# Values right behind the scores, and a last chunk of tokens at full height, in a fused attention and mixer kernel

## The chip, the cores and the metric

The kernel runs on one core of a Trainium2 chip. The core has five engines with queues of their own: TensorE (PE, with its weight loads as PEld), VectorE (DVE), ScalarE (ACT), GpSimd (POOL) and SyncE (SP), which here only issues DMAs. Each engine works through its instructions in the order in which the program emits them; semaphores hold an instruction back until its inputs are there. The metric is the time of one execution in device microseconds, as the median over several runs.

## The reference

Attention with a threshold, then an MLP mixer. All results are float32; the four MLP weights arrive as float64, because a float32 array is multiplied with a float64 scalar.

```python
# q, k, v: (8, 8, 576, 64); tau = 0.02
scores = scale * np.matmul(q, k.transpose(0, 1, 3, 2))
thresh = np.max(scores, axis=-1, keepdims=True) - tau
scores = np.where(scores >= thresh, scores, -1000000000.0)
scores = scores - np.max(scores, axis=-1, keepdims=True)
attn = np.exp(scores)
attn = attn / (np.sum(attn, axis=-1, keepdims=True) + 1e-09)
x = np.matmul(attn, v)                     # then (B, H, S, D) -> (B, S, H*D) = (8, 576, 512)
...
h = np.maximum(x.transpose(0, 2, 1) @ w_tok1, 0.0) @ w_tok2     # 576 -> 256 -> 576 tokens
u = x + h.transpose(0, 2, 1)
out = u + np.maximum(u @ w_ch1, 0.0) @ w_ch2                    # 512 -> 1536 -> 512 channels
```

## The kernel before

The work is cut into 144 units: 8 batch rows, in each of them two groups of two head pairs, in each group 9 units (`t` 0 to 8). A unit is 128 query rows of one head pair; unit `t == 4` holds the last 64 query rows of both pairs. One loop (from line 524) goes over the units and emits, by hand and in this order, what each engine is to do; nothing is reordered afterwards.

In one turn of the loop for unit `u` stand:

- `scores(u)`: TensorE computes the scores of both heads into PSUM (`sc`, line 297, two matmuls in the two halves of the array at a time, shape 64*128); VectorE takes the row maximum (`mx`, line 302), GpSimd makes the bias (line 303). From row 1 on `sc` has one pair of buffers.
- `norm(u - 1)`: VectorE makes the reciprocal of the row sums (lines 321 and 322), GpSimd scales the exponentials (line 325).
- `turn_blocks(u - 2)` (from row 1 on) or `turn` (row 0): the weights of attention are transposed. In row 0 TensorE does it, with copies out of PSUM (line 350). From row 1 on VectorE transposes blocks of 32x32 (line 359), and when a group of one or two units is complete, SyncE issues 16 DMAs that move the blocks from `T` to `eT` (line 369). The group's call of `values` is then put on the list `due`, for two units later (one in row 0).
- `fill(share)`: takes steps of the two MLPs from the list `todo`, up to a share of a quota per unit. A step is a handful of matmuls and what follows them: `turn_x` (lines 423 and 424), `tok1` (433 and 434), `tok2` (440 and 444), `ch1` (462 and 463), `ch2` (474 to 484). MLP results go through PSUM tiles with two buffers.
- `weigh(u)`: ScalarE applies the threshold (line 312) and the exponential with the row sum (line 315).
- the calls of `values` that are due: TensorE multiplies `eT` with v (`pv`, lines 399 and 404, shape 128*64), ScalarE copies the result to `xT` (line 409). When the last call of a batch row is done, `push` puts that row's MLP steps on `todo` and sets the quota.
- loads of later q, k and v, and `prep`, which transposes q and k on VectorE (line 279).

Each float32 matmul appears in the trace as two instructions.

The float64 weights come as pairs of 32-bit words, in 31 pieces. A piece is loaded into one of `NRAW` areas of a tile that only later serves as `xT`, and converted by integer operations: two on ScalarE (lines 187 and 189), three on VectorE (lines 197, 201 and 205), one on GpSimd (line 211). Before, this runs as a pipeline in steps, three to a piece: step 3i emits GpSimd's addition for piece i - 1, the next load into the freed area, and VectorE's first operation on piece i; the two others emit one operation of ScalarE for piece i + 1 and one of VectorE for piece i. In row 0 `weight(1)` is called twice a unit; from row 1 on `weight(2)` three times: behind `norm`, ahead of `weigh`, and behind `values`. `need` emits what an MLP step is missing. 36 of the 93 steps fall in row 0.

The queue of SyncE holds, in the order emitted, the loads of pieces (line 172), in row 0 q and k (106), v (114), the block transfers (369) and the results (484). From row 1 on q and k are loaded from ScalarE's queue.

576 tokens are 4 chunks of 128 and one of 64. `tok1` contracts over tokens, so its fifth chunk uses 64 rows of the array (shape 64*128 at line 433).

Of the kernel before, what the change touches and what calls it, by code (L numbers as in the profile page):

```python
# [9 lines left out]
F32 = mybir.dt.float32  # L10
U32 = mybir.dt.uint32
I32 = mybir.dt.int32
# [5 lines left out]
P = 128  # L18
# [3 lines left out]
def kernel(  # L22
# [103 lines left out]
    wc1 = const.tile([P, NJ, NCC, P], F32, name="wc1")  # L126
    wc2 = const.tile([P, NJ, DM], F32, name="wc2")

    WMAX = 512
    scratch = work.tile([P, NP * 2 * S], U32, tag="xT", name="scratch")
    NRAW = 4
    raw_at = [scratch[:, 2 * WMAX * i : 2 * WMAX * (i + 1)] for i in range(NRAW)]

    def like(x, dst):
# [14 lines left out]
    for j in range(NJ):  # L152
        pieces.append((wc2[:, j, :], moe_w_ch2[P * j : P * j + P, :]))

    raws = {}

    def load_piece(i):
        if i >= len(pieces):
            return
# [5 lines left out]
        raw = raw_at[i % NRAW][0:rows, 0 : n * (2 if wide(i) else 1)].bitcast(src.dtype)  # L171
        nc.sync.dma_start(out=like(raw, dst), in_=src)
        if wide(i):
            words = raw.bitcast(U32).rearrange("p (n w) -> p n w", w=2)
            h2 = work.tile([P, WMAX], F32, tag="o", name=f"h2_{i}")[0:rows, 0:n]
            raws[i] = like(words[:, :, 0], dst), like(words[:, :, 1], dst), like(h2, dst)
        else:
            raws[i] = like(raw, dst)

    def wide(i):  # L180
        return i < len(pieces) and pieces[i][1].dtype == I64

    def on_scalar(i, part):
        if wide(i):
            lo, hi, h2 = raws[i]
            if part == 0:
                nc.scalar.activation(out=lo.bitcast(I32), in_=lo, func=AF.Copy, scale=2.0**-29)
            else:
                nc.scalar.activation(out=h2, in_=hi.bitcast(F32), func=AF.Square)

    def on_vector(i, part):
        if wide(i):
            dst = pieces[i][0]
            lo, hi, h2 = raws[i]
            bits = dst.bitcast(U32)
            if part == 0:
                nc.vector.tensor_scalar(
                    out=bits, in0=hi, scalar1=3, scalar2=0x3FFFFFFF, op0=ALU.logical_shift_left, op1=ALU.bitwise_and
                )
            elif part == 1:  # L200
                nc.vector.scalar_tensor_tensor(
                    out=bits, in0=hi, scalar=0xC0000000, in1=bits, op0=ALU.bitwise_and, op1=ALU.bitwise_or
                )
            else:
                nc.vector.scalar_tensor_tensor(out=dst, in0=h2, scalar=2.0**-30, in1=dst, op0=ALU.is_ge, op1=ALU.mult)

    def on_gpsimd(i):
        if i >= 0:
            dst = pieces[i][0]
            if wide(i):  # L210
                nc.gpsimd.tensor_tensor(out=dst.bitcast(I32), in0=dst.bitcast(I32), in1=raws.pop(i)[0].bitcast(I32), op=ALU.add)
            else:
                nc.gpsimd.tensor_copy(out=dst, in_=raws.pop(i))

    steps_done = 0

    def weight(n):

        nonlocal steps_done
        for k in range(steps_done, min(steps_done + n, 3 * len(pieces) + 1)):
            i, part = divmod(k, 3)
            if part == 0:
                on_gpsimd(i - 1)
                if i:
                    load_piece(i - 1 + NRAW)
            else:
                on_scalar(i + 1, part - 1)
            on_vector(i, part)  # L230
            steps_done = k + 1

    def need(i):

        weight(3 * i + 4 - steps_done)

    load_piece(0)
    load_qk(1, (nc.sync, nc.sync))
# [1 line left out]
    for i in range(1, NRAW):  # L240
        load_piece(i)
    load_v(1)
    on_scalar(0, 0)
    on_scalar(0, 1)

# [166 lines left out]
    def token_mlp(b):  # L412
        xT = xTs.pop(b)
        o = S * (b % 2)
        s = {}

        def turn_x(t):
            M = MT[t]
            if t == 0:
                s["x"] = work.tile([P, NT, DM], F32, tag="x", bufs=1, name=f"x_{b}")  # L420
            ps = ps_tr.tile([P, MAIN], F32, tag="tr", name=f"tx_{b}_{t}").rearrange("p (c x) -> p c x", c=NP)
            for p in range(NP):
                nc.tensor.transpose(out=ps[0:M, p, :], in_=xT[:, p, o + t * P : o + t * P + M], identity=ident)  # L423
            nc.scalar.copy(out=s["x"][0:M, t, :], in_=ps[0:M].rearrange("q p d -> q (p d)"))

        def tok1(m):
            need(2)
            if m == 0:
                s["a"] = work.tile([P, NTK, DM], F32, tag="a", bufs=1, name=f"a_{b}")
            ps = ps_mm.tile([P, DM], F32, tag="mm", name=f"t1_{b}_{m}")  # L430
            for t in range(NT):
                M = MT[t]
                nc.tensor.matmul(ps, lhsT=w1[0:M, t, P * m : P * m + P], rhs=s["x"][0:M, t, :], start=(t == 0), stop=(t == NT - 1))  # L433
# [74 lines left out]
    def push(b):  # L508
# [102 lines left out]
```

## Time and profile before

| what | value |
|---|---|
| time, median of 3 runs (lowest to highest) | 1412.02 us (1411.59 to 1416.25) |
| the profiled execution: its time, its span | 1412.02 us, 1410.2 us |
| mean granted clock of TensorE | 0.984 |
| PE busy, 0 to 50, 50 to 100, 100 to 150, 150 to 200 us | 32.5, 37.0, 33.5, 45.3 us |
| DVE busy in the same stretches | 30.7, 41.9, 42.2, 37.3 us |
| PE busy, 600 to 800 us | 199.9 us of 200 |
| chain that ended last, by engine | PE 81%, DVE 6%, SP queue 5%, DMA 3%, ACT 3% |
| block transfers eT<-T: issues, length of one issue (median), issue to landing | 1120, 588 ns, about 2 us |
| first max of unit 18 (row 1), 36 (row 2), 54 (row 3), 143 | 102.9, 277.3, 415.2, 1207.2 us |

Times in the profile are microseconds from the start of the span, unless marked ns. A line of a timeline gives the start, the length, the engine, the line of the kernel, the operation, what it writes and reads, and how many instructions were merged; in square brackets stands how long the engine was idle before and what ended that. SPq and ACTq are DMA issues in the queues of SyncE and ScalarE. Ends of matmuls are modelled, so distances between their starts are what can be compared. The span is a little shorter than the execution's time.

### The profile page before, as it was taken

To read this page: it belongs to the slowest core of one execution; us is meant where nothing else is said; L and a number is where in the kernel's file an instruction comes from. 1 tells how busy PE (TensorE), PEld (TensorE's weight loads), DVE (VectorE), ACT (ScalarE), POOL (GpSimd) and SP (SyncE) were. 2 spreads that over 40 slices of the span, in tenths; PEclk is the share of its full clock that TensorE was granted. 3 is DMA by queue.
4 is the path that set the end of the run, shared out by engine and by line. 5 is a ranking of instruction groups with operands and counts; after the bars stand their busy time and mean duration, and the time that the engine had idled before them with its cause. 6 is when DMAs were issued, how large, how long until landed. Compare 5 with 4: busy or idle time off the path is not lost.

```text
span 1410.2 us, 19481 instructions
## 1 busy us (share of the span) xinstructions
PE 1338.3 (95%) x6866; PEld 828.3 (59%) x6866; DVE 585.2 (41%) x1009; ACT 588.8 (42%) x1328; POOL 358.9 (25%) x681
## 2 busy tenths in 40 slices
PE   5767799979999999999999999999999999999998
PEld 3443556536665567565756566565656466566675
DVE  5788673344444443434333444434333443201000
ACT  5776554344445444353334344443334344220110
POOL 4566552222222222222122222212212222100000
PEclk8998999989999999999999999999999999999999
DMA  6444654443444434433333434342443433300000
GB/s 133 103 104 115 170 136 110 106 101 92 118 117 105 107 87 101 104 93 93 90 95 83 111 81 116 91 109 68 99 94 77 111 90 79 88 8 16 8 8 23
DMA packets 257376, 128.34 MB, mean 91 GB/s; under 512 B 208064, under 2 KB 221376, under 8 KB 257280
## 3 DMA queue, kind: packets, MB, share of 16 engines
q1 hardware_dynamic: 131632, 111.46, 30.0%
q10 hardware_dynamic: 125648, 15.64, 7.0%
q8 instruction: 55, 0.90, 0.3%
q14 instruction: 41, 0.34, 0.1%
HBM read 43.25 MB, written 9.44 MB: 37 GB/s over the span
## 4 chain that ended last, share of the span: by engine, by line
PE 81%; DVE 6%; SPq 5%; DMA 3%; ACT 3%; issue 1%; POOL 1%; DVEq 0%; ACTq 0%
PE c L478 27%; PE c L462 23%; PE sc L297 10%; PE pv L404 7%; SPq L369 4%; PE t L433 4%; PE t L440 3%; DVE mx L302 3%; PE pv L399 2%; DVE T L359 2%; PE tx L423 1%; DMA eT<-T 1%; PE c L474 1%; ACT e L312 1%; ACT e L315 1%
## 5 line engine op out<-in xcount | busy, mean ns | idle before, releaser
L302 DVE TENSOR_REDUCE mx<-sc 128x1 f32<-128x576 f32 x288 | 204.7, 751 | 495.2 <-PE sc L297 493.2
L462 PE MATMUL c<-xT,wc 128*128 128x256 f32 (+1 forms) x1920 | 405.7, 363 | 3.1 <-ACT g L463 1.8
L478 PE MATMUL c<-wc,g 128*128 128x512 f32 x864 | 389.5, 597 | 0.0
L462 PEld LDWEIGHTS c<-xT,wc 128*128 128x128 f32 x1920 | 331.1, 190 | 76.9 <-issue 29.6
L303 POOL TENSOR_SCALAR bias<-mx,toff 128x1 f32<-128x1 f32 x288 | 79.6, 276 | 833.5 <-DVE mx L302 779.0
L312 ACT ACTIVATE e<-sc,bias 128x576 f32<-128x576 f32 x288 | 199.2, 740 | 168.3 <-POOL bias L303 156.3
L478 PEld LDWEIGHTS c<-wc,g 128*128 128x128 f32 x864 | 157.6, 190 | 177.3 <-issue 175.6
L463 ACT ACTIVATE g<-c 128x256 f32<-128x256 f32 (+1 forms) x240 | 86.9, 363 | 383.5 <-PE c L462 372.4
L325 POOL TENSOR_SCALAR e<-e,rr 128x576 f32<-128x576 f32 x288 | 219.6, 775 | 16.6 <-DVE rr L322 4.4
L315 ACT ACTIVATE e<-e,ntau 128x576 f32<-128x576 f32 x288 | 220.2, 772 | 0.0
L297 PE MATMUL sc<-kT,qT 64*128 64x288 f32 (+1 forms) x1280 | 191.9, 435 | 14.7 <-DVE kT L279 8.7
L359 DVE STREAM_TRANSPOSE T<-e 128x1152 f32<-128x1152 f32 x126 | 172.5, 1369 | 15.8 <-DMA eT<-T 10.0
L297 PEld LDWEIGHTS sc<-kT,qT 64*128 64x128 f32 (+1 forms) x1280 | 104.8, 179 | 95.7 <-issue 51.1
L404 PE MATMUL pv<-eT,lv 128*64 128x256 f32 x1024 | 125.8, 389 | 0.0
L483 DVE COPY o<-c 128x512 f32<-128x512 f32 x36 | 24.6, 684 | 192.6 <-PE c L478 192.6
L404 PEld LDWEIGHTS pv<-eT,lv 128*64 128x64 f32 x1024 | 76.5, 141 | 38.3 <-issue 2.8
L440 PE MATMUL t<-w,a 128*128 128x288 f32 x256 | 78.0, 434 | 13.9 <-DVE xT L444 12.1
L433 PE MATMUL t<-x,w 128*128 128x512 f32 (+1 forms) x160 | 74.9, 606 | 0.0
L409 ACT COPY xT<-pv 128x256 f32<-128x256 f32 x64 | 23.8, 372 | 115.1 <-PE pv L404 114.9
L440 PEld LDWEIGHTS t<-w,a 128*128 128x128 f32 x256 | 46.9, 197 | 38.4 <-DVE xT L444 17.0
L444 DVE TENSOR_TENSOR xT<-xT,t 128x288 f32<-128x288 f32 x64 | 27.9, 441 | 97.5 <-PE t L440 97.4
L315 ACT ACTIVATION_READ_ACCUMULATOR e<-e,ntau 128x1 f32 x288 | 57.0, 198 | 0.0
(46 smaller groups left out, 600.9 us busy)
## 6 DMA issues: line engine op xcount, KB each, us to landing
eT<-T SPq DMA_DIRECT2D x896, 72.0 KB, 2.1
scratch<-in_moe_w_ch_dram SPq DMA_DIRECT2D x24, 512.0 KB, 3.8
lv<-in_v_dram SPq DMA_DIRECT2D x32, 288.0 KB, 3.3
out_dram<-o SPq DMA_DIRECT2D x36, 256.0 KB, 2.2
eT<-T SPq DMA_DIRECT2D x224, 36.0 KB, 1.9
lk<-in_k_dram ACTq DMA_DIRECT2D x108, 72.0 KB, 2.7
lq<-in_q_dram ACTq DMA_DIRECT2D x104, 72.0 KB, 2.1
lq<-in_q_dram SPq DMA_DIRECT2D x24, 72.0 KB, 3.3
```

What stands on the lines that cost most here:

```text
L297: nc.tensor.matmul(sc[h][rows, f, 0:HS], lhsT=qT[r, cols], rhs=kT[r, HS * f : HS * f + HS], start=True, stop=True)
L302: nc.vector.tensor_reduce(out=mx[:, c], in_=sc[h][:, :, 0:HS], axis=AX.XY, op=ALU.max)
L312: nc.scalar.activation(out=eh, in_=sc[h][:, :, 0:HS], func=AF.Prelu, bias=bias[:, h : h + 1], scale=SCALE, alpha=STEEP)
L315: nc.scalar.activation(out=eh, in_=eh, func=AF.Exp, bias=ntau, accum_out=rs[:, h : h + 1])
L325: nc.gpsimd.tensor_scalar(out=eh, in0=eh, scalar1=rr[:, h : h + 1], scalar2=1.0, op0=ALU.mult, op1=ALU.mult)
L359: nc.vector.transpose(out=T.rearrange("p (a c n x) -> p c a n x", a=4, c=NK, n=n)[:, :, :, place, :], in_=e.rearrange("p (c a x) -> p c a ...
L404: nc.tensor.matmul(to[r], lhsT=lv[:, j, :], rhs=eT[:, j], start=False, stop=(c == NI - 1), skip_group_check=True)
L433: nc.tensor.matmul(ps, lhsT=w1[0:M, t, P * m : P * m + P], rhs=s["x"][0:M, t, :], start=(t == 0), stop=(t == NT - 1))
L440: nc.tensor.matmul(ps, lhsT=s["a"][:, m, P * c : P * c + P], rhs=w2[:, m, HS * f : HS * f + HS], start=(m == 0), stop=(m == NTK - 1))
L462: nc.tensor.matmul(ps, lhsT=wc1[:, j, c, :], rhs=uT[:, c, GR * i : GR * i + n], start=(c == 0), stop=(c == NCC - 1))
L463: nc.scalar.activation(out=s["g"][:, j, 0:n], in_=ps, func=AF.Relu)
L478: nc.tensor.matmul(flat, lhsT=s["g"][:, j, P * t : P * t + P], rhs=wc2[:, j, :], start=False, stop=(j == NJ - 1), skip_group_check=True)
```

## The change

Three things change.

1. From row 1 on, the calls of `values` that are due are emitted directly behind `scores(u)`, by the new function `mix`. In row 0 they stay where they were.
2. The result of `turn_x` goes to a tile `x_sb` that lasts for the whole kernel and whose fifth chunk is zero in its lower 64 rows; `w1` gets zeros there too. `tok1` contracts all five chunks over 128 rows. Two memsets on GpSimd write these zeros at the start.
3. The conversion of weights is a generator: all operations of a piece belong to its own three steps (ScalarE's two with VectorE's first; VectorE's second; VectorE's third, GpSimd's addition and the next load). It works in two scratch areas and one for the squares, in the same tile, with three areas for raw loads in place of four. In row 0 there are still two steps a unit; from row 1 on four ahead of `weigh` and three at the end, none behind `norm`.

```diff
+    x_sb = const.tile([P, NT, DM], F32, name="x_sb")
+    nc.gpsimd.memset(x_sb[LAST:P, NI, :], 0.0)
+    nc.gpsimd.memset(w1[LAST:P, NI, :], 0.0)
...
-    NRAW = 4
+    NRAW = 3
+    a_at = [scratch[:, 2 * WMAX * NRAW + WMAX * i : 2 * WMAX * NRAW + WMAX * (i + 1)] for i in range(2)]
+    sq_at = scratch[:, 2 * WMAX * NRAW + 2 * WMAX : 2 * WMAX * NRAW + 3 * WMAX].bitcast(F32)
...
+    def f64_to_f32(dst, raw, rows, n):
+        lo, hi = raw[:, :, 0], raw[:, :, 1]
+        a = a_at[turn_of[0] % 2][0:rows, 0:n]
+        h2 = sq_at[0:rows, 0:n]
+        turn_of[0] += 1
+        af = a.bitcast(F32)
+        nc.scalar.activation(out=lo.bitcast(I32), in_=lo, func=AF.Copy, scale=2.0**-29)
+        nc.scalar.activation(out=h2, in_=hi.bitcast(F32), func=AF.Square)
+        yield nc.vector.tensor_scalar(
+            out=a, in0=hi, scalar1=3, scalar2=0x3FFFFFFF, op0=ALU.logical_shift_left, op1=ALU.bitwise_and
+        )
+        yield nc.vector.scalar_tensor_tensor(
+            out=a, in0=hi, scalar=0xC0000000, in1=a, op0=ALU.bitwise_and, op1=ALU.bitwise_or
+        )
+        nc.vector.scalar_tensor_tensor(out=af, in0=h2, scalar=2.0**-30, in1=af, op0=ALU.is_ge, op1=ALU.mult)
+        nc.gpsimd.tensor_tensor(
+            out=dst.bitcast(I32), in0=like(a.bitcast(I32), dst), in1=like(lo.bitcast(I32), dst), op=ALU.add
+        )
...
+    def weight_ops():
+        for i, (dst, src) in enumerate(pieces):
+            raw, rows, n = raws.pop(i)
+            if src.dtype == I64:
+                for _ in f64_to_f32(dst, raw.bitcast(U32).rearrange("p (n w) -> p n w", w=2), rows, n):
+                    yield
...
+            if i + NRAW < len(pieces):
+                load_piece(i + NRAW)
+            yield
...
-    on_scalar(0, 0)
-    on_scalar(0, 1)
...
-            nc.scalar.copy(out=s["x"][0:M, t, :], in_=ps[0:M].rearrange("q p d -> q (p d)"))
+            nc.scalar.copy(out=x_sb[0:M, t, :], in_=ps[0:M].rearrange("q p d -> q (p d)"))
...
-                M = MT[t]
-                nc.tensor.matmul(ps, lhsT=w1[0:M, t, P * m : P * m + P], rhs=s["x"][0:M, t, :], start=(t == 0), stop=(t == NT - 1))
+                nc.tensor.matmul(ps, lhsT=w1[:, t, P * m : P * m + P], rhs=x_sb[:, t, :], start=(t == 0), stop=(t == NT - 1))
...
+    def mix(u):
+        while due and due[0][0] <= u:
+            _, b, p, c = due.popleft()
+            values(b, p, c)
+            if p == NP - 1 and c == 1:
+                push(b)
...
         if on:
             scores(u)
+        if b_now:
+            mix(u)
         if 0 < u <= len(units):
             norm(u - 1)
-        if b_now:
-            weight(2)
...
         if b_now:
             fill(0.4)
-        weight(2 if b_now else 1)
+        weight(4 if b_now else 1)
         if on:
             weigh(u)
         if b_now:
             fill(0.3)
-        while due and due[0][0] <= u:
-            _, b, p, c = due.popleft()
-            values(b, p, c)
-            if p == NP - 1 and c == 1:
-                push(b)
+        if not b_now:
+            mix(u)
         if b_now:
             fill(0.3)
-        weight(2 if b_now else 1)
+        weight(3 if b_now else 1)
...
-    need(len(pieces) - 1)
+    weight(10000)
```

More of the change, by code (lines that the diff above doesn't have):

```diff
@@ L127 @@
     wc2 = const.tile([P, NJ, DM], F32, name="wc2")
+    x_sb = const.tile([P, NT, DM], F32, name="x_sb")
+    nc.gpsimd.memset(x_sb[LAST:P, NI, :], 0.0)
+    nc.gpsimd.memset(w1[LAST:P, NI, :], 0.0)
     WMAX = 512
     scratch = work.tile([P, NP * 2 * S], U32, tag="xT", name="scratch")
-    NRAW = 4
+    NRAW = 3
     raw_at = [scratch[:, 2 * WMAX * i : 2 * WMAX * (i + 1)] for i in range(NRAW)]
+    a_at = [scratch[:, 2 * WMAX * NRAW + WMAX * i : 2 * WMAX * NRAW + WMAX * (i + 1)] for i in range(2)]
+    sq_at = scratch[:, 2 * WMAX * NRAW + 2 * WMAX : 2 * WMAX * NRAW + 3 * WMAX].bitcast(F32)
+    turn_of = [0]
     def like(x, dst):
@@ L163, in load_piece @@
     def load_piece(i):
-        if i >= len(pieces):
-            return
         dst, src = pieces[i]
@@ L170, in load_piece @@
             n *= d
-        raw = raw_at[i % NRAW][0:rows, 0 : n * (2 if wide(i) else 1)].bitcast(src.dtype)
+        wide = src.dtype == I64
+        raw = raw_at[i % NRAW][0:rows, 0 : n * (2 if wide else 1)]
+        raw = raw.bitcast(src.dtype)
         nc.sync.dma_start(out=like(raw, dst), in_=src)
[L173 to L187, printed above, removed]
-            else:
[L189 to L213, printed above, removed]
+        raws[i] = raw, rows, n
+    def weight_ops():
[4 more added lines that the diff above has]
+                    yield
+            else:
+                yield
+                yield
+                nc.gpsimd.tensor_copy(out=dst, in_=like(raw, dst))
+            if i + NRAW < len(pieces):
+                load_piece(i + NRAW)
+            yield
@@ L217 @@
+    wops = weight_ops()
     steps_done = 0
@@ L221, in weight @@
         nonlocal steps_done
[L222 to L231, printed above, removed]
+        for _ in range(n):
+            if next(wops, wops) is wops:
+                return
+            steps_done += 1
     def need(i):
-        weight(3 * i + 4 - steps_done)
+        weight(3 * i + 3 - steps_done)
     load_piece(0)
@@ L418, in turn_x @@
             M = MT[t]
-            if t == 0:
-                s["x"] = work.tile([P, NT, DM], F32, tag="x", bufs=1, name=f"x_{b}")
             ps = ps_tr.tile([P, MAIN], F32, tag="tr", name=f"tx_{b}_{t}").rearrange("p (c x) -> p c x", c=NP)
```

## The prediction, made before the changed kernel was run

> **What bounds the kernel now.** I read the page first, then the windows of 20 to 200 us, the gaps of TensorE, and for three stretches the timeline and the chain of waits.
>
> ```profile
> span 1410.2 us, 19481 instructions
> PE 1338.3 (95%) x6866; PEld 828.3 (59%) x6866; DVE 585.2 (41%) x1009; ACT 588.8 (42%) x1328; POOL 358.9 (25%) x681
> ...
> PE   5767799979999999999999999999999999999998
> ```
>
> TensorE is busy in 9 tenths or more of nearly every slice after the seventh (247 us). So from there on only three things count: the time that TensorE loses inside its own stream, waits that stop it, and what is left undone before. Summed over the trace, gaps of TensorE above 0.3 us come to 58.3 us, of which 21.4 us lie before 100 us (row 0), 21.2 us between 100 and 200 us (row 1, where the weights are still converted), 10.7 us between 250 and 350 us, and only about 5 us in all the rest.
>
> Inside the stream, the timeline of TensorE near the end shows what a change of the array's shape costs. Columns: start, length, then the group.
>
> ```profile
> 1236.19 1.89 PE L462 MATMUL c<-xT,wc 128*128 128x256 f32 x8
> 1238.01 0.65 PE L399 MATMUL pv<-eT,vl 128*64 128x256 f32 x4
> ...
> 1242.59 1.89 PE L462 MATMUL c<-xT,wc 128*128 128x256 f32 x8
> 1244.31 0.60 PE L423 MATMUL tx<-ident,xT 128*128 128x128 f32 x4
> ...
> 1252.98 4.65 PE L433 MATMUL t<-x,w 128*128 128x512 f32 x10
> 1257.56 1.99 PE L462 MATMUL c<-xT,wc 128*128 128x256 f32 x8
> ```
>
> The same eight matmuls take 1.82 us from start to start when a 128*64 group follows and 1.72 us when a 128*128 group follows. Over all such pairs between 450 and 1200 us the medians are 309 against 216 ns for a 256-column matmul and 522 against 429 ns for a 512-column one: **93 ns for each change of shape**. The token group (L433) takes 4.58 us where ten full matmuls would take 4.29 us: its last chunk (64 rows) costs a change in, 533 ns in place of 429 ns between its two passes, and a change out.
>
> Two waits of TensorE matter for this change. Shown are SyncE's queue, TensorE some 10 us later, and then unit 20 on TensorE and ScalarE.
>
> ```profile
> 410.60 29.46 SPq L369 DMA_DIRECT2D eT<-T  x33
> ```
>
> ```profile
> 420.48 1.24 PE L297 MATMUL sc<-kT,qT 64*128 64x288 f32 x8
> 421.65 1.99 PE L462 MATMUL c<-xT,wc 128*128 128x256 f32 x8
> 424.47 0.65 PE L399 MATMUL pv<-eT,vl 128*64 128x256 f32 x4 [0.83 <-DMA eT<-T]
> ```
>
> ```profile
> 117.77 0.65 PE L399 MATMUL pv<-eT,vl 128*64 128x256 f32 x4
> ...
> 122.92 0.68 ACT L187 ACTIVATE scratch<-scratch 128x512 int32<-128x512 uint32 x1 [3.51 <-DMA scratch<-in_moe_w_ch_dram]
> ...
> 126.81 0.36 ACT L409 COPY xT<-pv 128x256 f32<-128x256 f32 x1
> ...
> 127.22 3.76 PE L423 MATMUL tx<-ident,xT 128*128 128x128 f32 x16 [6.48 <-ACT xT L409]
> ```
>
> First: SyncE issues the 16 block transfers of a group (L369) at about 0.63 us each, so a group takes 10 us, lands 1.5 us later, and pv waits for the last. Second: in unit 20, the first with MLP work, the copy of pv sits on ScalarE behind a conversion that waits for its raw load and behind weigh; TensorE stands for 6.48 us.
>
> **The change part by part.** Units are counted 0 to 143, row 1 begins with unit 18.
>
> Values behind scores: a call moves 20 matmuls, 20 weight loads and one ScalarE copy (372 ns for 256 columns) ahead of turn_blocks, weigh, the weight steps and 0.7 of the unit's fill. No DMA is in it. TensorE's order per unit goes from scores, MLP, values, MLP to scores, values, MLP: one change of shape fewer where MLP stood on both sides. Of the 72 runs of pv after 100 us, 46 have MLP on both sides, two of these in the tail without scores; the others touch the next scores (22), scores (3) or a half-height group, and keep their count. 44 x 93 ns = **-4.1 us** (-5 to -3).
>
> The full-height chunk: 16 token groups. Followed by pv (8 of them) each has one change and 104 ns less, 197 ns, in one case 290; the three between MLP work save 290 ns each. Those followed by scores save nothing: at 620.80 us such a group and the scores behind it take 5.55 us, and ten full passes, a change and scores (4.29 + 0.09 + 1.17) take 5.55 us too, because scores of the other half run beside the half-height pass. 7 x 0.197 + 0.29 + 3 x 0.29 + 0.3 for the rest = **-2.8 us** (-4 to -2). [...]
>
> The moved wait: values of unit u now come right behind scores(u), some 4.4 us earlier, and want a group whose transposes ran in unit u-2. For each of the 68 groups with scores in the unit of its values I subtracted the landing of its last transfer from the end of these scores. Before, the median distance from landing to pv is 6.4 us; to the end of scores it is 2.0 us, and ten are below zero, 15.9 us together. For the pv at 424.47 shown above: landing 424.1, scores end 421.7, so 2.4 us late. One of the ten (-4.0 us, unit 39) costs nothing, since TensorE already stands there for 4.15 us with its MLP list empty. The six others that matter fall in units 46 to 57, where a unit lasts only 6.5 to 8 us. A wait in unit u pushes later scores and, for groups queued behind another group, gives SyncE time; carried through, the waits are 1.2 + 0.6 + 1.8 + 1.7 + 0.7 + 0.2 = 6.2, less the 0.9 already paid: **+5.3 us**. Everywhere else 14 groups land less than 1 us ahead of the need; the changes saved tighten these: **+1.5 us**. Lower end of both +3; upper end, landing 1 us later throughout: 33.1 in place of 15.9, so +20.
>
> Behind the waiting pv stand, on TensorE, the unit's MLP; on ScalarE, behind its copy, the unit's weigh (3.4 us: two at 740, two at 772, two reads at 198 ns). Who waits for weigh: the next scores, since sc has one pair of buffers. Scores 1.17, values 2.3, fill 0.4 x 6 and a Relu copy 0.4 put Prelu at 6.3 and its end at 7.7 us, before the next scores at 8.9: no cost while the MLP fills that gap; without it up to 1.5 us a unit.
>
> Tail: values in unit 145 lose 5 us of cover against a distance of 4.3: **+0.7 us** (0 to 1.5).
>
> Row 0: the number of instructions per piece is the same (ScalarE 2, VectorE 3, GpSimd 1) and so are two steps a unit. ScalarE's two of a piece now come with that piece's first step instead of one piece ahead. In unit 1 this takes Copy and Square of piece 1 (waiting for a load that lands at 15.57, then 1.23 us) from ahead of Prelu(1): **-1.5 us** (-3 to +3; plus where both stand ahead of a weigh that the chain passes). One load fewer in the prologue spares SyncE 0.58 us; two memsets on GpSimd (205 ns for 128 columns, so up to 1.2 us) lie in its idle time before the first bias, at 12 us.
>
> Row 1: (a) unit 20's gap. The copy now stands ahead of conversion and weigh: **-6.5 us**. (b) Seven steps a unit for six: VectorE's conversion (650 + 932 + 783 ns a piece) grows from 4.7 to 5.5 us a unit and ends in unit 26, not 27. VectorE was 17 to 18 of every 20 us busy from 100 to 140, so units stretch, then fewer are stretched: **+2.5 us** (-2 to +6). (c) Waits for raw loads: ScalarE stood 16.0 us on them before, load 7 steps ahead; it is 7 steps again, now one unit in place of 1.17. Loads that SyncE queues behind a group (units 21, 23, 24) land some 18 us after that unit's first max (3.2 to the end of its transposes, 10.1 for the group, 4.7 for issue and landing), and are wanted about 15 us after (a unit of 10.5 and 4.5 into the next): 3 x 3 = 9 us, against 9.1 us that TensorE lost on VectorE's and ScalarE's lateness in units 22 to 26 before (4.38, 2.93, 1.80). **0** (-4 to +10; VectorE's last step now may also stand for ScalarE's Square in the same slot). Row 1: **-4.0 us**.
>
> Sum: -4.1 - 2.8 + 5.3 + 1.5 + 0.7 - 1.5 - 4.0 = -4.9 us. The profiled execution took 1412.02 us (span 1410.2 and 1.8 around it), which is also the median of the three. 1412.0 - 4.9 = **1407 us**.
>
> [...] The trace shows 0.83 granted from 100 to 140 us, around the 6.48 us gap, and 1.00 through 400 to 600 us with gaps below 1 us. [...]
>
> **The rivals.**
> Waits take the drains' place. For it: 24 of 68 groups have under 1 us. Against it: from unit 58 on only 7.6 us are lost even if all land 1 us later. Then +7.6 for the +1.5: 1413 us. Here belongs also that the order saves no change (three scores-to-pv neighbours in the trace: 332 ns, as scores to MLP): 1411.
> Row 1 gets slower (the other side): conversion, now in one slot, holds VectorE and ScalarE together on a load behind a block transfer. Price: 9 us of (c) not replacing the old loss but added, and +6 in (b): 1407 + 9 + 3.5 = 1419 us. It decides from about 9 us of extra TensorE gap between 120 and 200 us. For it: 10 us of issue before a load of 3.8 us; against it: before paid this too.
> Transfers late throughout, by 2 us: 24 us after unit 57 and more before: 1430 us.
>
> **How the numbers follow.** A measurement of this kernel can tell 0.3%, 4.2 us. Small gain (forecast, own range 1397 to 1408): 0.44. Cancelled, 1408 to 1416: 0.27. Row 1 slower: 0.19. Transfers late: 0.10. So faster 0.44, same 0.27, slower 0.29. The range: unknowns taken together reach some 10 us down and 17 up, 1397 to 1424; beyond lie mostly the last rival's times.
>
> **What would show it.** pv directly behind sc in TensorE's timeline with 93 ns between shapes; L433 groups of 4.29 us; the 6.48 us gap gone; DMA waits of pv near 11 us (5.0 before), mostly between 290 and 440 us. I am wrong if these waits pass 20 us, or if unit 28's first max comes later than 205 us: it came at 204.9.

## The result, and the profile after

The changed kernel takes 1432.19 us (median of 6 runs, 1429.75 to 1434.82), the kernel before in the same session 1413.70 us (6 runs). The ratio is 1.0132, with an interval of 1.0115 to 1.0148: slower by 18.5 us, outside the range of the prediction. The profiled execution took 1433.63 us, its span is 1431.8 us.

The page of the changed kernel:

```profile
span 1431.8 us, 19564 instructions
...
PE 1343.2 (94%) x6866; PEld 843.0 (59%) x6866; DVE 585.0 (41%) x1009; ACT 586.0 (41%) x1328; POOL 347.9 (24%) x683
...
PE   6777889978999999999999999999999999999998
```

The same 6866 matmul instructions are there, yet TensorE is busy 4.9 us longer, and the slice from 322 us on, at 9 tenths or more before, stands at 8. To see where the 21.6 us of span come from, the trace is cut at three first maxima (units 18, 36, 60) and at unit 143. These windows stand below, first of the kernel before, then of the changed one. Columns: the window, its length, then for each engine busy time and instructions, and after POOL the granted clock of TensorE, the DMA share and GB/s.

```profile
102.90:277.30 174.40, 153.19 (x774) 93.75 (x771) 107.80 (x170) 88.78 (x191) 76.76 (x100) 0.94 0.48 126
277.30:460.90 183.60, 171.97 (x909) 103.06 (x909) 84.15 (x142) 87.47 (x194) 50.16 (x106) 0.97 0.45 108
460.90:1207.20 746.30, 741.53 (x3867) 456.89 (x3867) 301.88 (x511) 314.93 (x726) 174.22 (x370) 1.00 0.39 94
```

```profile
102.10:287.60 185.50, 163.40 (x775) 100.07 (x772) 107.22 (x171) 88.84 (x190) 65.39 (x100) 0.90 0.45 120
287.60:485.10 197.50, 177.63 (x919) 108.69 (x919) 84.26 (x142) 87.33 (x195) 50.18 (x106) 0.96 0.44 103
485.10:1232.00 746.90, 735.35 (x3882) 462.30 (x3882) 302.96 (x512) 313.94 (x727) 174.20 (x370) 1.00 0.39 93
```

Two stretches make the loss. **Row 1** (units 18 to 35) is 11.1 us longer, **units 36 to 59** are 13.9 us longer. The long remainder to unit 143 costs 0.6 us, row 0 gives 0.8 and the tail 3.2 us. (E1 below has the row 0 of before, and its unit 18 comes at 104.1 us, not 102.9: the 0.8 us can't be told from nothing.) In row 1 hardly any of the 11.1 us is idle time: TensorE is busy 10.2 us longer with one instruction more, at a granted clock of 0.90 against 0.94. Followed in time, the clock in the trace is 0.50 for 37.5 us of the changed kernel's row 1 and for 20.5 us of row 1 before, and 1.00 for the rest. The matmuls of a token group (L423) start 854 ns apart from 138.59 us on, where the clock is 0.50, and 429 ns apart from 1275.32 us on, where it is 1.00. So half of the time for which TensorE is busy at 0.50 is counted as lost to the clock, an estimate: 15.6 us after and 8.1 us before, so that 7.5 of the 10.2 us are the clock. In units 36 to 59 it is idle 8.2 us longer and busy 5.7 us longer, with ten matmul instructions more; by the same estimate 3.3 of the 5.7 us are the clock (0.96 against 0.97 granted, 6.3 and 3.0 us lost).

Next come the lines that answer to those ahead of the prediction. TensorE in units without waits, and in the tail (start, length, group):

```profile
1060.62 1.24 PE L290 MATMUL sc<-kT,qT 64*128 64x288 f32 x8
1061.79 0.65 PE L392 MATMUL pv<-eT,vl 128*64 128x256 f32 x4
...
1064.10 0.66 PE L464 MATMUL c<-ident,xT 128*128 128x128 f32 x4
```

```profile
1273.59 1.89 PE L452 MATMUL c<-xT,wc 128*128 128x256 f32 x8
1275.32 4.46 PE L423 MATMUL t<-x_sb,w 128*128 128x512 f32 x10
1279.61 1.89 PE L452 MATMUL c<-xT,wc 128*128 128x256 f32 x8
```

Values stand behind scores, and a token group takes 4.29 us from start to start: both parts do what they say. After 100 us the changes of shape, counted by the shape that each matmul has in the trace, fall from 398 to 336 (381 with full height alone). 45 of the 62 come from the order, which was priced at 44; 62 x 93 ns are 5.8 us, and the 16 half-height passes save 104 ns each besides: together 7.4 us, close to the 6.9 us of the two terms -4.1 and -2.8.

Unit 20 and a group whose transfers are late:

```profile
120.46 1.12 PE L392 MATMUL pv<-eT,vl 128*64 128x256 f32 x4
121.36 3.45 PE L397 MATMUL pv<-eT,lv 128*64 128x256 f32 x16
124.74 3.29 PE L414 MATMUL tx<-ident,xT 128*128 128x128 f32 x20
124.86 0.38 ACT L402 COPY xT<-pv 128x256 f32<-128x256 f32 x1 [4.04 <-PE pv L397]
```

```profile
430.59 17.66 SPq L362 DMA_DIRECT2D eT<-T  x23
...
439.64 1.31 PE L290 MATMUL sc<-kT,qT 64*128 64x288 f32 x8
...
443.33 0.65 PE L392 MATMUL pv<-eT,vl 128*64 128x256 f32 x4 [2.38 <-DMA eT<-T]
```

The 6.48 us ahead of the first token transposes are gone, as forecast. In their place stands, in row 1, the lateness of weigh. Below is the worst place, with SyncE, ScalarE and TensorE together:

```profile
181.37 6.68 SPq L362 DMA_DIRECT2D eT<-T  x9
...
183.51 0.67 ACT L163 ACTIVATE scratch<-scratch 128x512 int32<-128x512 uint32 x1 [4.86 <-DMA scratch<-in_moe_w_ch_dram]
...
184.08 0.65 ACT L164 ACTIVATE scratch<-scratch 128x512 f32<-128x512 f32 x1
...
184.75 0.67 ACT L163 ACTIVATE scratch<-scratch 128x512 int32<-128x512 uint32 x1
...
185.51 0.68 ACT L164 ACTIVATE scratch<-scratch 128x512 f32<-128x512 f32 x1
...
186.09 1.36 ACT L305 ACTIVATE e<-sc,bias 128x576 f32<-128x576 f32 x2
186.86 1.80 PE L290 MATMUL sc<-kT,qT 64*128 64x288 f32 x4 [5.17 <-ACT e L305]
```

A raw load came late, ScalarE's Copy waits 4.86 us for it, two pieces are then converted, and only then weigh (L305) frees `sc`; TensorE stands for 5.17 us. In row 1 scores wait 16.2 us in all for weigh. The conversion's groups in row 1 show who waits for whom (busy time and mean ns, then the idle time before and its releasers):

```profile
L171 DVE SCALAR_TENSOR_TENSOR scratch<-scratch 128x512 f32<-128x512 f32 x20 | 14.7, 736 | 15.3 <-ACT scratch L164 13.6 <-ACT e L308 0.5 <-DVE scratch L168 0.5
L163 ACT ACTIVATE scratch<-scratch 128x512 int32<-128x512 uint32 x19 | 12.7, 671 | 11.4 <-DMA scratch<-in_moe_w_ch_dram 11.4
L164 ACT ACTIVATE scratch<-scratch 128x512 f32<-128x512 f32 x19 | 12.7, 666 | 6.6 <-DVE scratch L171 6.6
L165 DVE TENSOR_SCALAR scratch<-scratch 128x512 uint32<-128x512 uint32 x19 | 8.3, 438 | 7.7 <-DMA scratch<-in_moe_w_ch_dram 7.7
```

ScalarE's Square (L164) and VectorE's last step (L171) wait for each other: the one for the only area of squares, the other for the square of its own piece. And VectorE, which lost 0.6 us on raw loads before (100 to 220 us), loses 7.7 us on them now.

### The profile page after: what moved, and what is told of

Same layout as the page of the kernel before. It is cut to its first block, busy times and chain, and to the rows that moved or that the text cites. A ratio compares the mean times of both kernels' runs of the same rounds, so it can differ in the third digit from the quotient of the medians.

```text
span 1431.8 us, 19564 instructions
## 1 busy us (share of the span) xinstructions
PE 1343.2 (94%) x6866; PEld 843.0 (59%) x6866; DVE 585.0 (41%) x1009; ACT 586.0 (41%) x1328; POOL 347.9 (24%) x683
## 4 chain that ended last, share of the span: by engine, by line
PE 75%; SPq 8%; DVE 7%; DMA 4%; ACT 3%; issue 2%; POOL 1%; ACTq 0%; DVEq 0%; POOLq 0%
PE c L452 23%; PE c L468 22%; PE sc L290 9%; SPq L362 8%; PE pv L397 7%; PE t L423 5%; PE t L430 3%; DVE mx L295 3%; PE pv L392 2%; DMA eT<-T 2%; DVE T L352 1%; ACT e L305 1%; PE tx L414 1%; DMA lk<-in_k_dram 1%; PE c L464 1%
## 5 line engine op out<-in xcount | busy, mean ns | idle before, releaser
L305 ACT ACTIVATE e<-sc,bias 128x576 f32<-128x576 f32 x288 | 198.3, 740 | 97.0 <-POOL bias L296 95.2
L290 PE MATMUL sc<-kT,qT 64*128 64x288 f32 (+1 forms) x1280 | 198.3, 445 | 31.9 <-ACT e L305 22.7
L318 POOL TENSOR_SCALAR e<-e,rr 128x576 f32<-128x576 f32 x288 | 214.1, 756 | 14.4 <-DVE rr L315 1.6
L290 PEld LDWEIGHTS sc<-kT,qT 64*128 64x128 f32 (+1 forms) x1280 | 109.5, 184 | 124.4 <-issue 53.4
L352 DVE STREAM_TRANSPOSE T<-e 128x1152 f32<-128x1152 f32 x126 | 172.5, 1369 | 16.1 <-DMA eT<-T 11.0
L397 PE MATMUL pv<-eT,lv 128*64 128x256 f32 x1024 | 130.4, 399 | 0.0
L397 PEld LDWEIGHTS pv<-eT,lv 128*64 128x64 f32 x1024 | 80.9, 144 | 38.2 <-issue 5.8
L473 DVE COPY o<-c 128x512 f32<-128x512 f32 x36 | 24.5, 681 | 181.1 <-PE c L468 181.0
L423 PE MATMUL t<-x_sb,w 128*128 128x512 f32 x160 | 73.7, 608 | 0.0
L392 PE MATMUL pv<-eT,vl 128*64 128x256 f32 x256 | 43.6, 419 | 20.0 <-DMA eT<-T 15.4
```

The lines of the kernel that those rows point to most:

```text
L290: nc.tensor.matmul(sc[h][rows, f, 0:HS], lhsT=qT[r, cols], rhs=kT[r, HS * f : HS * f + HS], start=True, stop=True)
L305: nc.scalar.activation(out=eh, in_=sc[h][:, :, 0:HS], func=AF.Prelu, bias=bias[:, h : h + 1], scale=SCALE, alpha=STEEP)
L318: nc.gpsimd.tensor_scalar(out=eh, in0=eh, scalar1=rr[:, h : h + 1], scalar2=1.0, op0=ALU.mult, op1=ALU.mult)
L352: nc.vector.transpose(out=T.rearrange("p (a c n x) -> p c a n x", a=4, c=NK, n=n)[:, :, :, place, :], in_=e.rearrange("p (c a x) -> p c a ...
L397: nc.tensor.matmul(to[r], lhsT=lv[:, j, :], rhs=eT[:, j], start=False, stop=(c == NI - 1), skip_group_check=True)
L423: nc.tensor.matmul(ps, lhsT=w1[:, t, P * m : P * m + P], rhs=x_sb[:, t, :], start=(t == 0), stop=(t == NT - 1))
```

## The experiments

Each kernel was measured beside the kernel before. Row 1 is the time from the first max of unit 18 to that of unit 36, "36 to 59" from there to unit 60, both from one profile of each kernel. E3, E7, E11 and E12 are the same program up to unit 36, and their row 1 takes 169.4 to 170.7 us: differences of about 1.3 us in that column can't be read.

| kernel | median us | ratio to before (95%) | row 1 | 36 to 59 |
|---|---|---|---|---|
| before | 1412 to 1415 | | 174.4 | 183.6 |
| changed | 1432.19 | 1.0132 (1.0115 to 1.0148) | 185.5 | 197.6 |
| E1 order alone | 1423.53 | 1.0072 (1.0047 to 1.0096) | 170.6 | 198.9 |
| E2 full height alone | 1409.03 | 0.9971 (0.9958 to 0.9984) | 172.8 | 184.6 |
| E3 order and height | 1419.96 | 1.0051 (1.0033 to 1.0069) | 169.4 | 200.7 |
| E4 conversion alone | 1420.22 | 1.0054 (1.0035 to 1.0074) | 185.2 | 183.6 |
| E5 changed, two squares | 1430.68 | 1.0125 (1.0103 to 1.0147) | 181.3 | 201.3 |
| E6 changed, weigh first | 1431.05 | 1.0128 (1.0109 to 1.0147) | 183.9 | 198.5 |
| E7 E3, no order in 36 to 59 and the tail | 1404.37 | 0.9938 (0.9921 to 0.9955) | 170.6 | 183.3 |
| E8 values behind the last fill, height | 1401.76 | 0.9922 (0.9904 to 0.9939) | 169.9 | 180.8 |
| E9 E3, new places of the steps | 1428.36 | 1.0123 (1.0107 to 1.0138) | 178.4 | 199.8 |
| E10 changed, old storage, weigh first | 1427.18 | 1.0110 (1.0094 to 1.0125) | 177.7 | 198.5 |
| E11 E8, but E3's order in row 1 | 1399.78 | 0.9910 (0.9897 to 0.9923) | 170.7 | 178.9 |
| E12 E3, values one unit later in 37 to 59 | 1403.27 | 0.9942 (0.9926 to 0.9957) | 170.6 | 176.2 |
| E13 E3, seven steps | 1430.23 | 1.0123 (1.0107 to 1.0139) | 177.6 | 200.5 |
| E14 E3, four steps ahead of weigh | 1425.30 | 1.0091 (1.0076 to 1.0106) | 174.5 | 198.2 |
| E15 changed, old places and rate | 1431.41 | 1.0134 (1.0112 to 1.0156) | 184.5 | 198.3 |
| E16 E15, old storage | 1420.17 | 1.0046 (1.0031 to 1.0062) | 168.7 | 199.1 |
| E17 E15, two squares | 1426.95 | 1.0091 (1.0070 to 1.0112) | 179.1 | 199.9 |
| E18 E15, four raw areas | 1424.97 | 1.0079 (1.0060 to 1.0097) | 173.0 | 197.0 |

**The parts of the change (E1 to E4).** Each takes its hunks of the diff onto the kernel before: E1 and E3 the first fence, E2 and E3 the second, E4 the generator of the conversion with its places.

```diff
             scores(u)
+        if b_now:
+            mix(u)
...
-        while due and due[0][0] <= u:
+        if not b_now:
+            mix(u)
```

```diff
-                nc.tensor.matmul(ps, lhsT=w1[0:M, t, P * m : P * m + P], rhs=s["x"][0:M, t, :], start=(t == 0), stop=(t == NT - 1))
+                nc.tensor.matmul(ps, lhsT=w1[:, t, P * m : P * m + P], rhs=x_sb[:, t, :], start=(t == 0), stop=(t == NT - 1))
```

> Values behind scores alone, conversion and half-height chunk as before. Theory A (the slowdown in row 1 is the conversion's: its single area for squares makes ScalarE wait for VectorE ahead of weigh): gaps of TensorE on scores waiting for ScalarE stay below 8 us, row 1 (first max of unit 18 to that of unit 36) within 4 us of before; pv's waits for transfers rise from 5 to some 15 us in rows 1 to 3, about 45 shape changes fewer give back 4 us: 3 to 8 us slower in all. Theory B (the order itself is to blame in row 1: pv and its copy hold weigh back): row 1 10 us or more longer, and the whole 10 to 20 us slower.

> Full-height last chunk alone. Both theories: 1.5 to 3.5 us faster, the L433 groups 4.29 us from start to start of what follows plus one change of shape, where before has 4.58; nothing else moves.

> Values behind scores and full height, conversion as before (the change without its conversion part). Theory A: within 0 to 5 us of before, row 1 as before. Theory B: most of the 18 us of the whole change, 12 us or more slower.

> The changed conversion alone, values and chunk as before. Theory A: 8 to 14 us slower, all of it between the first max of unit 18 and that of unit 36, with 12 us or more of TensorE waiting for ScalarE ahead of scores. Theory B: within 4 us of before.

The order alone is slower by 10.1 us (1423.53 - 1413.45): it shortens row 1 by 3.8 us and lengthens units 36 to 59 by 15.3. The height alone gives 4.4 us. The conversion alone costs 6.8 us; in its profile row 1 is 10.8 us longer, and everything behind row 1 takes what it took before. The parts add up to 12.5 us, the whole is 18.5: with the old conversion order and height shorten row 1 by 5.0 us (174.4 to 169.4), with the new one not at all (185.2 and 185.5).

**Units 36 to 59 (E7, E8, E11, E12).** E7 puts values back to their late place there and in the tail:

```diff
-        if b_now:
+        early = b_now and u < len(units) and not 36 <= u < 60
+        if early:
             mix(u)
```

> Values behind scores and full height with the conversion of before, but in units 36 to 59 and in the tail the calls of values stay where they were before. Theory T (the order loses where units are short and the list of MLP steps is thin, by waits for transfers and weigh behind them): pv's waits for transfers between units 36 and 60 back to 5 us; 8 to 12 us faster than with the order everywhere, 1407 to 1412 us. Rival (the order loses evenly in all rows): 2 to 4 us faster than with it everywhere.

Against E3 the ratio falls from 1.0051 to 0.9938, some 16 us. The tail is no shorter for it (198.6 and 198.2 us), so the order costs that much in units 36 to 59. Two causes were possible: late transfers, or weigh behind the values' copy on ScalarE. E12 keeps the place and gives the transfers a unit more:

```diff
-                when = u + (2 if in_blocks(b) else 1)
+                when = u + (3 if 37 <= u < 60 else 2 if in_blocks(b) else 1)
```

> Order and full height with the conversion of before, and in units 37 to 59 each group's values one unit later, so that its block transfers have a unit more; the place directly behind the scores is kept. If the late transfers make the 15.6 us between order in those units (1420.0) and not (1404.4), the waits of pv on DMA between 290 and 460 us fall from 12.6 to below 3 us and the time comes to 1405 to 1408. If it is that weigh stands behind the values' copy on ScalarE, the idle time of the scores on e stays at 5 us and the time above 1413.

Groups of TensorE between the first maxima of units 36 and 60, first E3, then E12:

```profile
L301 PE MATMUL sc<-kT,qT 64*128 64x288 f32 (+1 forms) x218 | 33.3, 437 | 4.9 <-ACT e L316 4.9
L408 PE MATMUL pv<-eT,lv 128*64 128x256 f32 x176 | 26.3, 449 | 0.0
L403 PE MATMUL pv<-eT,vl 128*64 128x256 f32 x44 | 8.2, 452 | 12.6 <-DMA eT<-T 12.6
```

```profile
L301 PE MATMUL sc<-kT,qT 64*128 64x288 f32 (+1 forms) x216 | 34.5, 458 | 6.9 <-ACT e L316 6.9
L408 PE MATMUL pv<-eT,lv 128*64 128x256 f32 x160 | 19.6, 388 | 0.0
L403 PE MATMUL pv<-eT,vl 128*64 128x256 f32 x42 | 7.4, 429 | 0.8 <-DMA eT<-T 0.8
```

The wait for transfers falls from 12.6 to 0.8 us and the ratio from 1.0051 to 0.9942, some 15 us, though scores wait 2.0 us longer for weigh. So the late transfers are the cause; the place ahead of weigh alone costs little. The price is larger than the wait: without it a pv matmul takes 388 ns in the mean, with it 449. The granted clock is lower too, 0.95 in these units in E3 and 0.97 in E12: by the estimate above TensorE loses 8.4 and 4.0 us to it. How much of pv's 61 ns is the clock was not measured. E12 also moves MLP work to later units (from unit 60 to 143 it needs 753.7 us, E3 746.2), so the 24.5 us that units 36 to 59 gain are not all saved.

E8 takes the other way (first fence): the call of `values` goes behind the unit's last fill, right ahead of the next scores, with full height and the conversion of before. E11 (second fence) is E8 with the early place in row 1 alone.

```diff
+        if b_now:
+            fill(0.3)
         while due and due[0][0] <= u:
...
-        if b_now:
-            fill(0.3)
```

```diff
+        early = UB <= u < 2 * UB
+        if early:
+            mix(u)
...
+        if not early:
+            mix(u)
```

> Conversion of before, full height, and the calls of values moved the other way: behind the unit's last MLP steps, so that the next scores follow them. This saves the same change of shape, with 2 us more for the transfers instead of 6 us less. If shape changes are worth what was read (93 ns each, some 45 of them), and only the waits spoilt the order: 3 to 5 us faster than full height alone, 1404 to 1407 us. If the change count isn't what pays: same as full height alone, 1409 us.

> Values directly behind the scores in row 1 alone (units 18 to 35), from row 2 on behind the unit's last fill, full height, conversion of before. Values at the unit's end alone gave 1401.8, and behind the scores alone unit 36 came at the same 271.4 us. If row 1 gains from neither place, it is the same as 1401.8 within 3 us.

Both beat both kernels. E8 is some 7 us faster than E2 (0.9922 and 0.9971 of before), from which it differs in the order alone, with the same 336 changes of shape as the changed kernel, and pv waits 1.9 us for transfers in units 36 to 59. Values touch scores from either side; behind the fill they also have all of the unit's MLP as cover. E11 and E8 can't be told apart (1399.78 and 1401.76).

**Row 1, first guesses (E5, E6).** E5 gives the squares two areas, E6 puts the four steps behind weigh:

```diff
-        h2 = sq_at[0:rows, 0:n]
+        h2 = work.tile([P, WMAX], F32, tag="o", name=f"h2_{turn_of[0]}")[0:rows, 0:n]
```

```diff
-        weight(4 if b_now else 1)
+        if not b_now:
+            weight(1)
         if on:
             weigh(u)
+        if b_now:
+            weight(4)
```

> The changed kernel, with two areas for the squares (tiles of their own) in place of one. Theory A1 (with one area ScalarE's Square of a piece waits for VectorE's last step on the piece before, and weigh and the next scores behind it): TensorE's waits for ScalarE ahead of scores in row 1 fall from 16 to below 5 us, unit 36 comes 8 to 12 us earlier, the whole 1420 to 1424 us. Theory A2 (the conversion's operations stand ahead of weigh whatever area they use): less than 3 us gained.

> The changed kernel, with the four steps of conversion behind weigh in place of ahead of it, one area for squares. Theory A1: the wait of Square stays but holds nothing that scores need at once: 5 to 10 us gained. Theory A2: 8 to 12 us gained, no wait of scores for ScalarE above 5 us in row 1. Theory A3 (loads of raw pieces behind block transfers): below 3 us gained, and ScalarE's waits for loads stay at what the changed kernel has.

Neither moves the time by more than it can be measured. E6 removes the visible wait (scores wait 2.7 us for weigh in row 1, not 16.2), and row 1 gets just 1.6 us shorter, hardly more than profiles differ: token matmuls, transposes and pv wait instead, and ScalarE's Square now waits 11.4 us for VectorE's last step, with 6.6 us in the changed kernel. Removing the wait that ended last brought nothing: the conversion that fed it still ran late.

**Places, rate, form and storage (E9, E10, E13 to E18).** E9 runs the old pipeline at the new places; of its diff, shown below, E13 has the last hunk alone (seven steps at the old places), E14 the first two (four steps ahead of weigh, six in all). E10 is E6 with the storage of before: four raw areas, the result built in the weight's own bits, two areas for squares.

```diff
-        if b_now:
-            weight(2)
...
-        weight(2 if b_now else 1)
+        weight(4 if b_now else 1)
...
-        weight(2 if b_now else 1)
+        weight(3 if b_now else 1)
```

> Order and full height with the conversion of before (one piece ahead on ScalarE, result built in the weight's own bits, four raw areas), but its steps at the places of the changed kernel: none behind the norm, four ahead of weigh, three at the unit's end. If rate and place of the steps make row 1 slow, the first max of unit 36 comes near the changed kernel's 287.6 us and the time near 1430. If it is that one piece's operations on three engines stand in one slot, unit 36 stays within some 3 us of the 271.4 us that order and height gave with the old places, and the time near 1420.

> The changed kernel with all that its conversion lost in storage and place given back at once: two areas for the squares, four raw areas, the result built in the weight's own bits, the four steps behind weigh. Only that a piece's ScalarE, VectorE and GpSimd operations start in the same slot is kept. If storage and place together were the loss, unit 36 comes down from 287.6 us to about 272 and the time to about 1418. If the missing piece ahead is the loss, unit 36 stays above 282 us and the time above 1427.

> Order and full height, conversion of before at its old places, but seven steps a unit for six (two, two and three at the unit's end). If the rate is what delays row 1, the first max of unit 36 comes at about 280 us (271.4 without it) and the time near 1428. If the rate costs nothing, unit 36 stays at 270 to 273 us and the time near 1420.

> The same with six steps a unit, but none behind the norm, four in one go ahead of weigh and two at the end. If it is four steps in a row ahead of the weigh that delay row 1, unit 36 comes at about 280 us and the time near 1428. If the rate is the cause, unit 36 stays at 270 to 273 us.

With the old conversion each disturbs row 1: four steps ahead of weigh +5.1 us (174.5 against E3's 169.4), seven steps +8.2, both +9.0. Seven steps want each raw load sooner: in E13 ScalarE waits 20.6 us for raw loads between 100 and 220 us, in E3 17.3, and VectorE 5.6 against 3.6. E10 stays 8.3 us above E3: storage alone does not mend it while the steps do not stand where they did before.

E15 undoes those three hunks in the changed kernel. E17 adds E5's two squares to that, E18 the edit below, E16 both:

```diff
-    NRAW = 3
+    NRAW = 4
...
-        a = a_at[turn_of[0] % 2][0:rows, 0:n]
+        a = dst.bitcast(U32)
```

> The changed kernel with its steps at the places and the rate of before (two behind the norm, two ahead of weigh, two at the end); the new form of the conversion and its single area for the squares are kept. If places and rate make two thirds of the loss, unit 36 comes down from 287.6 us to 276 to 279 and the time to about 1422. If the form alone makes it, unit 36 stays above 284 us.

> The one-slot form at the old places and the old rate, with the storage of before (four raw areas, two areas for squares, the result built in the weight's own bits). If storage is what delays row 1, the first max of unit 36 comes at 270 to 275 us (271.4 with the old conversion, 287.2 with the new storage) and the time near 1420. If the missing piece ahead on ScalarE is it, unit 36 stays above 282 us and the time above 1427.

> Old places and rate, one-slot form, two areas for the squares; still three raw areas and the two areas of the intermediate result. If the single area for squares is the loss, the first max of unit 36 falls from 287.2 to 271 to 275 us and the time to about 1420; if it is the raw areas, unit 36 stays above 282 us.

> The same with four raw areas and the result built in the weight's own bits, and still one area for the squares. If the raw areas are the loss, unit 36 falls to 271 to 275 us and the time to about 1420; if it is the single area for squares, unit 36 stays above 282 us. If each is enough to hold the pipeline up, both runs stay above 280 us.

The old places and rate alone give nothing (184.5, 1431.41 us); with the old storage too, row 1 takes 168.7 us and the kernel 1420.17, as E3 does with the old conversion (169.4, 1419.96). So, given four raw areas, the **form costs nothing**: that all operations of a piece stand in one slot, with no piece ahead on ScalarE, is harmless then. (With four areas the new form loads a piece ten steps ahead, the old one seven to nine; the two at equal distance were not compared.) With the places of before the **storage** is the whole loss, and both halves of it count: with two squares and no more row 1 is still 9.7 us above E3, with four raw areas and one square 3.6 us. E18 also builds the result in the weight's bits; these two were not separated. The conversion's groups of E16 between 102 and 280 us:

```profile
L171 DVE SCALAR_TENSOR_TENSOR wc<-h,wc 128x512 f32<-128x512 f32 x20 | 14.8, 739 | 5.6 <-ACT h L164 4.8
L163 ACT ACTIVATE scratch<-scratch 128x512 int32<-128x512 uint32 x19 | 12.8, 673 | 1.5 <-DMA scratch<-in_moe_w_ch_dram 1.5
L164 ACT ACTIVATE h<-scratch 128x512 f32<-128x512 f32 x19 | 12.7, 667 | 0.0
L165 DVE TENSOR_SCALAR wc<-scratch 128x512 uint32<-128x512 uint32 x19 | 7.9, 416 | 3.4 <-DMA scratch<-in_moe_w_ch_dram 3.4
```

Against E15, which differs in storage alone, ScalarE's wait for raw loads falls from 13.6 to 1.5 us, VectorE's from 7.4 to 3.4, VectorE's wait for the Square from 10.9 to 4.8, and Square itself, which waited 5.3 us, waits no more. ScalarE's wait for loads alone is not the price: in E3 it is 17.3 us, more than in any of these, and row 1 is short. There ScalarE works a piece ahead, and VectorE waits just 3.6 us for loads and 2.6 us for the Square.

The prices do not add. Storage costs 15.8 us of row 1 at the old places (184.5 - 168.7), places and rate cost 9.0 with the old storage, all together 16.1. Once one holds the conversion up, the others find little left to hold; which of the two waits then decides a given unit was not followed further.

## Why the prediction was wrong

- **Row 1, the step "(c) Waits for raw loads"**, priced 0, failed; with it "(b) Seven steps a unit for six", +2.5. Together they measure +16.1 us (185.5 against E3's 169.4), the upper ends of their bounds, +10 and +6, added up. The step argued that "it is 7 steps again, now one unit in place of 1.17". That holds for ScalarE, which waits 11.4 us for loads where E3 has 17.3. VectorE's first operation had stood nine steps behind the load (issued in step 3i for piece i + 3), and now has seven; VectorE waits 7.7 us for loads where E3 has 3.6. In E16 and E18 four areas give both engines ten steps, and E18 alone takes back 11.5 of the 15.8 us that storage costs; how much of this is the distance and how much the result built in the weight's bits stays open. The same step named the wait of "VectorE's last step" for "ScalarE's Square" and left it in the range; its counterpart, the Square that waits for the only area, was not seen. E16 against E18 puts that area at 4.3 us.
- **What idle time costs.** The term set waits against waits: 9 us of new ones against 9.1 of old. Against E3, whose row 1 stands below, the new conversion adds 6.0 us of idle time (169.40 - 153.30 = 16.1 to 185.50 - 163.40 = 22.1) and 10.1 us of busy time:

```profile
102.00:271.40 169.40, 153.30 (x781) 94.39 (x775) 108.55 (x170) 88.06 (x191) 73.91 (x100) 0.97 0.48 128
```

  The granted clock of row 1 is 0.97 in E3 and 0.90 in the changed kernel: by the estimate above the one loses 4.4 us to it, the other 15.6, which covers the busy time. The sum held no term for that; the prediction has the clock for the stretch around unit 20's gap alone, and outside the sum.
- **The moved wait** was right in place and mechanism, and too small: +5.3 and +1.5 and +0.7 forecast. E7 against E3 puts it at some 16 us, E12 at some 15. The waits themselves are near the forecast: pv waits 15.4 us for transfers over the whole trace (2.6 of them in the tail), 5.0 before. What was left out is behind them: the clock (0.95 granted in E3, 0.97 in E12), with pv at 449 in place of 388 ns, and unit 39. "One of the ten (-4.0 us, unit 39) costs nothing, since TensorE already stands there for 4.15 us" is where this shows: the wait came, 3.73 us, but now values, their copy, the token copies and only then weigh stand behind it:

```profile
309.40 1.12 PE L392 MATMUL pv<-eT,vl 128*64 128x256 f32 x4 [3.73 <-DMA eT<-T]
310.28 2.88 PE L397 MATMUL pv<-eT,lv 128*64 128x256 f32 x16
...
313.19 0.37 ACT L402 COPY xT<-pv 128x256 f32<-128x256 f32 x1 [8.35 <-PE pv L397]
...
316.90 1.36 ACT L305 ACTIVATE e<-sc,bias 128x576 f32<-128x576 f32 x2
```

  Weigh starts 7.5 us behind pv, pv's sixteen matmuls take 2.88 us where 1.9 is usual, and units 38 and 39 take 22.1 us where they took 16.8 (first maxima 299.7 and 321.9; 290.1 and 306.9 before).

- **Weigh behind the copy**, "no cost while the MLP fills that gap": scores wait 5.0 us for weigh in units 36 to 59, 3.3 before, and 1.3 us after that. Nearly right, and E12 confirms that it is not the cause.
- **Right**: the changes of shape (45 from the order, forecast 44), the full height (4.4 us in E2, by its interval 2.3 to 5.9; -2.8 forecast) and unit 20's gap. **The tail** has the forecast wait, but 2.6 us of it where the term held +0.7; that it is 3.2 us shorter all the same, with TensorE busy 193.4 us in place of 199.2 because less work is left for it, is luck.
- **The rivals.** "Row 1 gets slower", at 1419 us, had the right mechanism, a conversion that holds VectorE and ScalarE together on a load behind a block transfer. It came together with the transfers of units 36 to 59, each about as large as that rival alone, where the prediction had taken one or the other. Its test, "about 9 us of extra TensorE gap between 120 and 200 us", did not show it, as the gap did not grow; "if unit 28's first max comes later than 205 us" did (218.4). "Transfers late throughout" did not come true: from unit 60 to 143 the stretch is 0.6 us longer.

## What to carry to other kernels

Count the slack of a prefetch separately for every engine that reads the buffer, and count scratch buffers as waits in both directions: storage cost 15.8 us of row 1 here (E15 and E16), and the one area for squares was 4.3 us of it. Where TensorE waits often, price its granted clock besides the waits (row 1 was granted 0.97 in E3, 0.90 in the changed kernel). A move that saves shape changes is worth most on the side of the neighbour where the moved work has cover: values ahead of the next scores gave the same 336 changes as values behind the last ones, and gained some 7 us where the other place lost 10. When the wait that ends last is removed and the time stays (E6), look for what feeds it.

## What the hardware showed that was not expected

Between two runs here, idle time was not all that waits cost TensorE. Row 1 of E15 and of E16, which differ in storage alone:

```profile
102.70:287.20 184.50, 161.36 (x775) 98.78 (x771) 104.47 (x171) 88.61 (x190) 69.17 (x100) 0.91 0.46 120
102.90:271.50 168.60, 155.26 (x775) 95.65 (x771) 101.92 (x170) 88.17 (x190) 71.99 (x100) 0.95 0.49 128
```

The same 775 matmuls take 6.1 us less, idle time falls by 9.8 us (184.50 - 161.36 = 23.1 to 13.3) and row 1 by 15.9: between these two a wait removed was worth 1.6 times its length. The granted clock is 0.91 in E15 and 0.95 in E16: by the estimate above E15 loses 13.0 us of busy time to it, E16 7.5, so 5.5 of the 6.1 us.

In the changed kernel one such stretch lies in the units behind row 1. The clock in the trace is 0.50 from 301.99 to 312.23 us, and 1.00 in the ten us before it and behind it. Before it, from 292.00 us on, TensorE is busy 6.29 of 9.99 us, with waits of 0.77, 1.10 and 2.59 us around the scores; in it 5.75 of 10.24 us; behind it, to 322.00 us, 9.48 of 9.77 us. The eight score matmuls at 302.75 us take 2.92 us, where the usual length is 1.24. A low busy share does not come with the lower clock everywhere: from 141.57 to 158.63 us TensorE is busy 10.91 of 17.06 us, and the clock is 1.00 throughout. What makes it fall was not shown by these runs.
